# Scores of the first two batches as unsplit float32 products, two heads side by side on the array's two row halves

## The chip, the cores and the metric

One core of one Trainium2 chip runs the whole program. The metric is the device time of one execution in microseconds (us). TensorE does the matrix products (PE in the profile, and PEld for its weight loads), VectorE (DVE) and ScalarE (ACT) do everything elementwise, GpSimd (POOL) only fills a few constants, and SyncE (SP) starts the DMA transfers. The engines run at the same time and wait for each other by semaphores. TensorE's clock has two levels here, 1.2 and 2.4 GHz; the profile's PEclk column is the share of the full clock that was granted.

## The reference

Block-causal attention feeds a squared-ReLU MLP, and that feeds a soft mixture of experts. Everything is float32.

```python
# attention: 8 batches, 8 heads, 576 tokens, head size 64; blocks of 64 tokens
scores = scale * np.matmul(q, k.transpose(0, 1, 3, 2))       # scale = 1/8
scores = np.where(block_i >= block_j, scores, -1000000000.0)
scores = scores - np.max(scores, axis=-1, keepdims=True)
attn = np.exp(scores)
attn = attn / (np.sum(attn, axis=-1, keepdims=True) + 1e-09)
x = np.matmul(attn, v)            # heads side by side: 4608 tokens x 512
# MLP, 512 -> 2048 -> 512
h = np.maximum(x @ w_in, 0.0)
x = h * h @ w_out
# soft mixture of 8 experts with 4 slots each
logits = x @ phi
slot_input = softmax_over_tokens(logits).T @ x
slot_out[e] = np.maximum(slot_input[e] @ w1[e], 0.0) @ w2[e]
out = softmax_over_slots(logits) @ slot_out
```

## The kernel before

**A recorded program.** The kernel does not issue instructions as it runs. Each step is recorded by `pr.add` with the engines that may do it, a cost in ns, a due time, what it reads and writes, and the PSUM group it needs. `Program.order` then plays the program forward with these costs and fixes the order of the instructions on every engine. The order in which an engine works is thus set by this planner; how long things take is only known from the profile.

**The stages.** Tokens come in chunks of 384. A slot is one chunk by one of 16 tiles of hidden units: `slot_h` multiplies x by a tile of w_in into bank HB (PE line L898), ACT squares the ReLU, and `slot_o` multiplies by a tile of w_out into the banks O (L923, 512 columns). Later chunks use a scheme with fewer products (L1137, L1165). These products are the bulk of PE's work, and each float32 factor in them is split into a high and a low fp32r part, so that three fp32r products stand for one float32 product. The 16 weight tiles arrive as 64-bit numbers and are decoded by ACT and DVE (`w_decode`, L809 to L822, into X, WQ, W and WL).

**Attention.** Batches 2 to 7 use `job64` (L461, L516), which the change leaves as it is but for what its loads wait for. Batches 0 and 1 use `job`, once for a pair of heads (h = 0, 1; p = 0 to 3) and a list `ti` of query tiles. Tile 0 holds 64 queries, tiles 1 to 4 hold 128 each, and tile i sees the first KV[i] = 64 + 128 i keys (h = 1 has its keys in reverse order of blocks). The jobs are [0,1,2,3] of batch 0, [4] of batch 0, [0,1] of batch 1 and [2,3,4] of batch 1, four pairs each.

In a job, q and k lie with the head's 64 numbers on the 128 partitions twice, because k and q come doubled from HBM (in_qk). The split form of the scores then works like this: ACT or DVE rounds k and q/8 to fp32r (L580, L583, L584), DVE subtracts to get the rest (L587 for k on the lower 64 partitions, L590 for q), all into the lane's tile R (aR, bR), and two fp32r products of 128 rows (L621, j = 0 and 1) sum to the float32 scores of one head. The [4] jobs were `plain` already: one unsplit float32 product per head on 128 doubled rows, which the profile shows as two passes.

After the scores DVE masks a corner (L642), takes the row maximum (L644), ACT takes the exponential and its sum (L662), DVE or ACT normalises (L679, L680, L706, L707), PE transposes the probabilities (L726), ACT or DVE copies them back (L730), and PE multiplies by v (L743, L753, L761).

Two lanes hold such a job: lane a (aR, aF, PSUM banks B, four of them) and, for two pairs of batch 0 at the start, lane b (bR, bF, banks O and HB, which the MLP does not need yet). When lane b is done, `swap` gives its memory to weight tiles 4 to 15. Lane a has two sets of inputs that take turns, one in aF and one in EX:

```python
sx, rkq, V_, VD_ = L.ins[L.z]
L.z = (L.z + 1) % len(L.ins)
```

Of the kernel before, what the change touches and what calls it, by code (L numbers as in the profile page):

```python
# [7 lines left out]
F32 = mybir.dt.float32  # L8
# [39 lines left out]
class Program:  # L48
# [50 lines left out]
    def order(self, banks):  # L99
# [9 lines left out]
        modes, mode = ([], [], [], []), 0  # L109
# [158 lines left out]
def emit(tc, qk, v, vd, kq2, v2, w, phi, w1, w2, jsel, gsel, out):  # L268
# [59 lines left out]
    NF = NV + 512 + 768 + 4 * S  # L328
    late = tc.alloc_tile_pool(name="lane_b", bufs=1)
    L0, L1 = Lane(), Lane()  # L330
    for L, pl_, nm in ((L0, cp, "a"), (L1, late, "b")):
        L.name, L.w = nm, "w" if L is L0 else "w1"
        L.R = pl_.tile([128, 6 * S], F32R, name=nm + "R")
        L.F = pl_.tile([128, 9216 if L is L0 else NF], F32, name=nm + "F")
        o = NV + 512 + 768
        L.rkq = L.F[:, o:o + 4 * S].rearrange("p (h n) -> p h n", h=2)
        L.hi = [L.R[:, 2 * S * h:2 * S * h + 2 * S] for h in range(2)]
        L.ql = [L.R[:, S * (4 + h):S * (5 + h)] for h in range(2)]
# [4 lines left out]
        if L is L0:  # L343
            x = EX[:, 0:4 * S + 512 + 768]
            L.ins.append(("2", x[:, 0:4 * S].rearrange("p (h n) -> p h n", h=2),
                          x[:, 4 * S:4 * S + 512].rearrange("p (h n) -> p h n", h=2),
                          x[:, 4 * S + 512:].rearrange("p (i n) -> p i n", i=6)))
        L.nm, L.sm, L.ri = (cp.tile([128, 12], F32, name=nm + x) for x in ("nm", "sm", "ri"))

    def lane_init(L):  # L350
        for x, _, _, VD in L.ins:
            pr.add(("pool", 600, lambda VD=VD: pool.memset(VD, 0.0)), w=[(L.name, "VD" + x)], due=-1)
        pr.add(("pool", 95, lambda: pool.tensor_copy(L.R[:, 5 * S - 64:5 * S], L.VD[:, 0, 0:64])),
               r=[(L.name, "VD")], w=[(L.name, "ql", 0)], due=-1)
        pr.add(("pool", 95, lambda: pool.memset(L.sm, 1.0)), w=[(L.name, "sm", i) for i in range(12)], due=-1)
        pr.add(("pool", 95, lambda: pool.memset(L.nm, 0.0)), w=[(L.name, "nm", i) for i in range(12)], due=-1)
# [32 lines left out]
    SG = [[[[(1, 0, 0, 192, 64)], [(2, 0, 0, 320, 0)]], [[(3, 0, 0, 448, 0)]], [[(4, 0, 0, 288, 0)], [(4, 1, 288, 288, 0)]]]]  # L389
    SG.append([[[(0, 0, 0, 64, 0), (1, 0, 0, 192, 64)], [(2, 0, 0, 320, 0)]]] + SG[0][1:])  # L390

# [21 lines left out]
    def a_r():  # L413
        if not aR:
            aR.append(cp.tile([128, 6 * S], F32, name="aR2", tag="aR"))
        return aR[0]
# [8 lines left out]
    def job64(b, p, due0, due1):  # L425
# [19 lines left out]
        oldR = idle([K(nm, h) for h in range(2) for nm in ("hk", "hq", "ql")])  # L445
        oldF = idle([K("PT", x) for x in range(NPT // 64)] + [K("P", h, i, z_) for h in range(2) for i in range(5) for z_ in parts(i)])
        pr.add(("sp", 50, lambda: sp.dma_start(kq(), kq2[n2])), w=[K("kq", z)], nbytes=8 * S * 128, after=oldR)
        pr.add(("sp", 50, lambda: sp.dma_start(v_2(), v2[n2])), w=[K("v2")], nbytes=8 * S * 128, after=oldR)
# [90 lines left out]
    def job(L, b, p, ti, due0, due1, plain=False, merge=True):  # L539
# [14 lines left out]
        nq = q1 - q0  # L554
        ks = [(0, k1), (S - k1, S)]
        sc, neg = (0.0625, 2 * NEG) if plain else (1.0, 0.125 * NEG)
        pi = hd // 2
        src = qk[hd:hd + 2].rearrange("h p n -> p h n")
        whole = q0 == 0 and k1 == S
        if whole:  # L560
            pr.add(("sp", 50, lambda: sp.dma_start(rkq, src)), w=[K("rk", h) for h in range(2)] +
                   [K("rq", h) for h in range(2)], nbytes=8 * S * 128 * 2)
        else:
            for h in range(2):
                a_, e_ = ks[h]
                pr.add(("sp", 50, lambda h=h, a_=a_, e_=e_: sp.dma_start(rkq[:, h, a_:e_], src[:, h, a_:e_])),
                       w=[K("rk", h)], nbytes=4 * k1 * 128)
# [1289 lines left out]
```

## Time and profile before

| | |
|---|---|
| three runs | 1181.99, 1182.32, 1183.26 us; median 1182.32 us |
| profiled execution, its own time | 1179.87 us |
| its span in the trace | 1178.1 us |
| mean granted clock of TensorE | 0.99 |
| busy: PE, DVE, ACT | 1130.9 us (96%), 862.0 us (73%), 642.0 us (54%) |
| DMA | 265.55 MB, mean 225 GB/s |

The shares are means over stages that differ: PE is busy nearly all of the time from 140 to 1140 us, while it is the other engines that are fullest before that. So the table is to be read stage by stage, with the rows further down. The span and the execution's own time differ by 1.8 us, which lie outside the program's instructions.

### The profile page before, as it was taken

What the parts mean: (1) busy time and instruction counts of PE and PEld (TensorE: products, weight loads), DVE (VectorE), ACT (ScalarE), POOL (GpSimd) and SP (SyncE); (2) the same over time, 40 slices, a digit from 0 to 9 for tenths busy, and PEclk for the clock granted to TensorE, in tenths of its full rate; (3) what the DMA queues carried; (4) which work ended last, traced back from release to release, by engine and by line L of the source; (5) the groups of instructions that cost most, each with busy time, mean ns of one, the idle gap of its engine ahead of it and who ended that gap; (6) DMA issues with size and microseconds to landing.
All of it is one profiled execution on the core that took longest, in us unless ns stands there. A gap on an engine that the chain in (4) does not pass through costs nothing.

```text
span 1178.1 us, 28641 instructions
## 1 busy us (share of the span) xinstructions
PE 1130.9 (96%) x10918; PEld 930.9 (79%) x10918; DVE 862.0 (73%) x2464; ACT 642.0 (54%) x2047; POOL 4.1 (0%) x17
## 2 busy tenths in 40 slices
PE   5889899999999999999999999999999999999995
PEld 4677687888888888888877888888877899779843
DVE  7999988988768777887888667878888766532202
ACT  6888787666555666645554656656664000122324
POOL 1000000000000000000000000000000000000000
PEclk9899999999999999999999999999999999999998
DMA  7598637778577954665576843756653866998889
GB/s 247 177 307 254 194 118 259 236 217 255 178 221 229 315 182 134 200 196 180 175 231 216 281 150 117 223 179 202 201 184 119 293 205 196 337 391 279 292 323 322
DMA packets 145769, 265.55 MB, mean 225 GB/s; under 512 B 18784, under 2 KB 72288, under 8 KB 145632
## 3 DMA queue, kind: packets, MB, share of 16 engines
q1 hardware_dynamic: 145632, 263.73, 68.9%
q8 instruction: 86, 1.41, 0.5%
q14 instruction: 51, 0.42, 0.1%
HBM read 222.78 MB, written 40.89 MB: 224 GB/s over the span
## 4 chain that ended last, share of the span: by engine, by line
PE 79%; DVE 7%; ACT 3%; DMA 3%; issue 1%; SPq 0%; DVEq 0%; ACTq 0%
PE O L1165 17%; PE HB L898 13%; PE O L923 13%; PE HB L1137 9%; PE B L1137 6%; PE B L461 6%; PE B L516 5%; PE B L1727 1%; PE B L1333 1%; ACT aF L478 1%; PE B L1386 1%; PE O L1691 1%; PE B L726 1%; PE B L753 1%; DVE anm L644 1%
## 5 line engine op out<-in xcount | busy, mean ns | idle before, releaser
L478 ACT ACTIVATE aF<-B,aF 128x192 f32<-128x192 f32 (+8 forms) x432 | 166.1, 416 | 55.0 <-DVE aF L473 39.4
L923 PE MATMUL O<-W,MG 128*128 128x512 f32 x600 | 178.3, 399 | 0.0
L1165 PE MATMUL O<-W,MG 128*128 128x512 f32 x576 | 168.5, 398 | 0.5 <-DVE MG L1149 0.5
L898 PE MATMUL HB<-MX,W 128*128 128x384 f32 x544 | 149.5, 346 | 4.3 <-ACT R L904 3.8
L471 DVE TENSOR_REDUCE aF<-B 128x1 f32<-128x192 f32 (+8 forms) x432 | 109.9, 315 | 39.2 <-PE B L461 37.9
L923 PEld LDWEIGHTS O<-W,MG 128*128 128x128 f32 x600 | 110.3, 188 | 19.7 <-issue 2.3
L1165 PEld LDWEIGHTS O<-W,MG 128*128 128x128 f32 x576 | 106.0, 188 | 22.8 <-issue 2.5
L898 PEld LDWEIGHTS HB<-MX,W 128*128 128x128 f32 x544 | 98.3, 189 | 13.1 <-ACT R L904 5.5
L508 DVE STREAM_TRANSPOSE aF<-aF 128x448 f32<-128x448 f32 (+8 forms) x216 | 98.4, 488 | 0.0
L478 ACT ACTIVATION_READ_ACCUMULATOR aF<-B,aF 128x1 f32 x432 | 98.2, 228 | 0.0
L904 ACT ACTIVATE R<-HB 128x384 f32<-128x384 f32 x96 | 47.6, 496 | 83.7 <-PE HB L898 80.9
L1165 PE MATMUL O<-WL,MG 128*128 128x512 f32 x288 | 89.3, 397 | 0.0
L923 PE MATMUL O<-WL,MG 128*128 128x512 f32 x264 | 77.7, 396 | 0.0
L461 PE MATMUL B<-aR 64*32 64x192 f32 (+8 forms) x3456 | 77.5, 302 | 0.0
L898 PE MATMUL HB<-MX,WL 128*128 128x384 f32 x224 | 76.9, 343 | 0.5 <-DVE WL L822 0.4
L461 PEld LDWEIGHTS B<-aR 64*32 64x32 f32 x3456 | 53.7, 105 | 27.2 <-issue 8.7
L898 PE MATMUL HB<-MXe,W 128*128 128x384 f32 x256 | 72.5, 343 | 0.6 <-ACT R L904 0.5
L907 DVE CAST MG<-R 128x384 fp32r<-128x384 f32 x73 | 26.0, 356 | 62.6 <-ACT R L905 61.8
L504 ACT ACTIVATE aF<-aF 128x256 f32<-128x256 f32 (+8 forms) x162 | 58.7, 432 | 19.3 <-DVE aF L498 19.3
L516 PEld LDWEIGHTS B<-aF,aR 64*64 64x64 f32 x1728 | 52.8, 133 | 17.3 <-issue 4.7
L516 PE MATMUL B<-aF,aR 64*64 64x192 f32 (+8 forms) x1728 | 65.3, 301 | 0.0
L1165 PEld LDWEIGHTS O<-WL,MG 128*128 128x128 f32 x288 | 53.9, 188 | 13.6 <-issue 1.9
(361 smaller groups left out, 2184.6 us busy)
## 6 DMA issues: line engine op xcount, KB each, us to landing
W<-ws_d SPq DMA_DIRECT2D x200, 256.0 KB, 3.3
WL<-wlo_d SPq DMA_DIRECT2D x83, 512.0 KB, 4.2
WL<-wlo_d SPq DMA_DIRECT2D x96, 256.0 KB, 3.0
aR<-in_kq SPq DMA_DIRECT2D x24, 576.0 KB, 4.6
aR<-in_v SPq DMA_DIRECT2D x24, 576.0 KB, 3.9
ws_d<-EX SPq DMA_DIRECT2D x16, 512.0 KB, 5.8
Wr<-in_w SPq DMA_DIRECT2D x16, 512.0 KB, 5.1
xt_d<-aF SPq DMA_DIRECT2D x8, 768.0 KB, 5.0
```

The source lines that it names most:

```text
L461: pe.matmul(bank(gs[h])[32 * g:32 * g + 32, c:c + 32 * i + 32].rearrange("p (b n) -> p b n", n=32), x[:, S + 64 * i + 32 * q_:S + 64 * i + ...
L471: pr.add(("dve", c_tt(n), lambda g=gs[h], n=n, c=c, x=x: dve.reduce_max(St[:, 0, x:x + 1], bank(g)[:, c:c + n], axis=AX.X, negate=True)), ...
L478: pr.add(("act", c_act(n, ext=2), lambda g=gs[h], n=n, c=c, x=x, i=i, h=h: act.activation(P_(i)[:, h], bank(g)[:, c:c + n], AF.Exp, bias=S ...
L504: act.activation(P_(i)[:, h], P_(i)[:, h], AF.Copy, scale=fct[:, x + h:x + h + 1])
L508: pr.add(("dve", c_tr(2 * n), lambda i=i: dve.transpose(P_(i), P_(i))), w=[K("P2", i, h) for h in range(2)])
L516: pe.matmul(bank(gs[q_])[64 * h:64 * h + 64, 32 * k:288].rearrange("p (i n) -> p i n", n=32), v_2()[sl, h, 64 * k:64 * k + 64], L0.F[sl, o ...
L898: pr.add(("pe", c_mm(CH), lambda a=a, b_=b_, sl=sl, n=n, k=k: pe.matmul(HB[:, 0:CH], (wl() if a == "l" else W[ft])[:, sl], b_(c, k), start ...
L904: pr.add(("act", c_act(CH), lambda: act.activation(r_, HB[:, 0:CH], AF.Relu)), w=["HB", ("r", j)], due=-1)
L907: pr.add([("dve", c_cp(CH), lambda: dve.tensor_copy(gh, r_)), ("act", c_act(CH, True), lambda: act.copy(gh, r_))], r=[("r", j)], w=[("gh", ...
L923: pr.add(("pe", c_mm(512), lambda a=a, b_=b_, sl=sl, t=t, p_=p_: pe.matmul(OB[t], a[:, sl], (wl() if b_ == "l" else W[ft])[:, 512:1024], s ...
L1137: pr.add(("pe", c_mm(CH), lambda a=a, b_=b_, k=k, fst=fst, lst=m == 5: pe.matmul((bank(g) if g else HB)[:, 0:CH], W[r][:, a + 128 * k:a + ...
L1165: pr.add(("pe", c_mm(512), lambda a=a, lo_=lo_, sl=sl, t=t, p_=p_: pe.matmul(OB[t], a[:, sl], wo(n) if lo_ else W[ft][:, 512:1024], start= ...
```

## The change

The split form is gone. For batches 0 and 1 the two heads of a pair now lie one above the other, head 0 on partitions 0 to 63 and head 1 on 64 to 127 (in_qk is no longer doubled), and each score tile is one float32 product per head with 64 rows, the two heads right after each other into two PSUM banks. Tile 0 uses 64 rows by 64 columns of the array, tiles 1 to 4 use 64 rows by 128 columns; `mode` 3 and 4 tell the planner of these. The scale of 1/8 moves into the exponential, so every group of maxima gets a small multiplication by 0.125, and tile 0 has its maximum and its exponential taken for each head apart, on 64 rows. The tiles aR and bR are gone; aR is now only `job64`'s input tile and exists from the start, so that the first loads of `job64` (in_kq, in_v) wait for nothing. Lane a gets a third set of inputs. The [4] jobs of batch 0 and the [0,1] jobs of batch 1 are recorded in turns (one pair of each), where all four [4] came first. A [4] job takes all four banks of its pool in one step, the other groups of tiles take two.

```diff
-        modes, mode = ([], [], [], []), 0
+        modes, mode = ([], [], [], [], []), 0
...
+def c_mm64(n):
+
+    return max(115.0, n / 0.6 + 5)
...
-        L.R = pl_.tile([128, 6 * S], F32R, name=nm + "R")
-        L.rkq = L.F[:, o:o + 4 * S].rearrange("p (h n) -> p h n", h=2)
+        L.rkq = L.F[:, o:o + 2 * S]
...
+            L.ins.append(("3", EX[:, 4 * S + 128:6 * S + 128], L.F[:, 8384:8896].rearrange("p (h n) -> p h n", h=2),
+                          L.F[:, 7616:8384].rearrange("p (i n) -> p i n", i=6)))
...
-        pr.add(("sp", 50, lambda: sp.dma_start(kq(), kq2[n2])), w=[K("kq", z)], nbytes=8 * S * 128, after=oldR)
-        pr.add(("sp", 50, lambda: sp.dma_start(v_2(), v2[n2])), w=[K("v2")], nbytes=8 * S * 128, after=oldR)
+        pr.add(("sp", 50, lambda: sp.dma_start(kq(), kq2[n2])), w=[K("kq", z)], nbytes=8 * S * 128, after=())
+        pr.add(("sp", 50, lambda: sp.dma_start(v_2(), v2[n2])), w=[K("v2")], nbytes=8 * S * 128, after=())
...
-        for h in () if plain else range(2):
-            raw, hi = rkq[:, h], L.hi[h]
-            a_, e_ = ks[h]
-            pr.add(cpy(hi[:, a_:e_], raw[:, a_:e_], k1), r=[K("rk", h)], w=[K("hk", h)], cls="hi")
-            pr.add(cpy_s(hi[:, S + q0:S + q1], raw[:, S + q0:S + q1], nq), r=[K("rq", h)], w=[K("hq", h)], cls="hi")
-            pr.add(sub(hi[64:128, a_:e_], raw[64:128, a_:e_], f(hi[64:128, a_:e_]), k1),
-                   r=[K("rk", h)], w=[K("hk", h)], cls="kl")
-            pr.add(sub_s(L.ql[h][:, q0:q1], raw[:, S + q0:S + q1], f(hi[:, S + q0:S + q1]), nq),
-                   r=[K("rq", h), K("hq", h)], w=[K("ql", h)], cls="ql")
...
+        def scores(gs, pieces):
+            def mm(ps):
+                for g, (i, c0, n, bc) in ps:
+                    for h in range(2):
+                        x, k0 = rkq[64 * h:64 * h + 64], (S - KV[i]) * h + c0
+                        rows = slice(0, 128) if i else slice(64 * h, 64 * h + 64)
+                        pe.matmul(bank(g[h])[rows, bc:bc + n], x[:, S + Q0[i]:S + Q0[i] + QW[i]], x[:, k0:k0 + n],
+                                  start=True, stop=True)
...
+        for ph_ in ([0, 1], [2], [3], [4]):
...
+            if tiles == [4]:
+                gs = [[Group(L.w) for _ in range(2)] for _ in range(2)]
+                scores(gs, [(4, 0, 288, 0), (4, 288, 288, 0)])
...
+            else:
+                gs = [Group(L.w) for _ in range(2)]
+                scores([gs] * len(tiles), [(i, 0, KV[i], 64 if i == 1 else 0) for i in tiles])
...
     for p in range(4):
         d = t_at(0) + 5 * p - 10
-        job(L0, 0, p, [4], d, d + 8.0, 1)
-    for p in range(4):
-        d = t_at(0) + 5 + 3 * p
-        job(L0, 1, p, [0, 1], d, d + 8.0, 0)
+        job(L0, 0, p, [4], d, d + 8.0)
+        job(L0, 1, p, [0, 1], d + 3, d + 11.0)
```

The planner makes a new order of everything from this. Three places show it. The first is the start of TensorE's program. Before, lanes a and b (aR, bR) take turns with split products: each line stands for a product with the high or the low part of q.

```order
L621 MATMUL B_69<-aR 128x192
L621 MATMUL B_70<-aR 128x320
L621 MATMUL B_71<-aR 128x64
L621 MATMUL B_69<-aR 128x192
L621 MATMUL B_70<-aR 128x320
L621 MATMUL B_71<-aR 128x64
L621 MATMUL O_65<-bR 128x192
```

After, the products read the loaded inputs themselves (aF, bF), head 0 and head 1 of a tile in successive lines and in different banks.

```order
L574 MATMUL B_69<-aF 64x64
L574 MATMUL B_70<-aF 64x64
L574 MATMUL B_69<-aF 128x192
L574 MATMUL B_70<-aF 128x192
L574 MATMUL O_65<-bF 64x64
L574 MATMUL O_66<-bF 64x64
L574 MATMUL O_65<-bF 128x192
L574 MATMUL O_66<-bF 128x192
L574 MATMUL B_71<-aF 128x320
L574 MATMUL B_72<-aF 128x320
```

Nothing stands ahead of the first score now but the loads, and tile 0 has moved to the front.

The second place is VectorE's program behind the last row maxima of the first two pairs (TENSOR_REDUCE) and ahead of the last normalisation of their probabilities (TENSOR_SCALAR on aF, 448 wide). Before, the split of the second two pairs (EX for lane a, bF for lane b) stands there:

```order
L644 TENSOR_REDUCE bnm<-O_66 128x1
L580 CAST aR<-EX 128x448
L580 CAST bR<-bF 128x448
L584 TENSOR_SCALAR aR<-EX 128x448
L587 TENSOR_TENSOR aR<-EX,aR 64x448
L668 TENSOR_SCALAR ari<-asm 128x1
L587 TENSOR_TENSOR bR<-bF,bR 64x448
L668 TENSOR_SCALAR bri<-bsm 128x1
L674 RECIPROCAL ari<-ari 128x1
L590 SCALAR_TENSOR_TENSOR aR<-EX,aR 128x448
```

After, the decoding of the first weight tile (X) stands in their place:

```order
L654 TENSOR_SCALAR bnm<-bnm 128x2
L769 TENSOR_SCALAR X_0_93<-X_0_93 128x512
L769 TENSOR_SCALAR X_1_94<-X_1_94 128x512
L614 TENSOR_SCALAR ari<-asm 128x2
L770 TENSOR_SCALAR X_0_93<-X_0_93 128x512
L616 RECIPROCAL ari<-ari 128x2
L770 TENSOR_SCALAR X_1_94<-X_1_94 128x512
L621 TENSOR_SCALAR aF<-aF,ari 128x448
```

So the splits have left the queue and the weights have moved up in it.

The third place is SyncE's queue of loads, from the first weight tile on (YA, call). Before:

```order
L790 DMA YA<-in_w 128x1024
L790 DMA call<-in_w 128x1024
L566 DMA aF<-in_qk 128x576 x2
L568 DMA aF<-in_qk 128x2x128
L1514 DMA J<-in_jsel 96x64
L576 DMA EX<-in_vd 64x3x64
L566 DMA EX<-in_qk 128x576 x2
L568 DMA EX<-in_qk 128x2x128
L790 DMA YA<-in_w 128x1024
```

After, further down in the same stretch, the first three loads of `job64` (aR) stand ahead of the second weight tile:

```order
L554 DMA aF<-in_qk 64x192 x2
L550 DMA bF<-in_qk 128x576
L556 DMA bF<-in_qk 128x448
L556 DMA aF<-in_qk 128x192
L444 DMA aR<-in_kq 128x1152
L445 DMA aR<-in_v 128x1152
L444 DMA aR<-in_kq 128x1152
L563 DMA aF<-in_vd 64x64
L1468 DMA J<-in_jsel 96x64
L746 DMA YA<-in_w 128x1024
```

The loads of q and k are halved in size, and `job64`'s have moved to the start of the program.

## Rows read from the trace of the kernel before

**Rows 1.** Windows: stretch, its us, busy us (instructions) by engine, PEclk, DMA share, GB/s.

```profile
0.00:20.00 20.00, 9.37 (x48) 8.54 (x49) 13.64 (x55) 13.28 (x37) 4.08 (x17) 1.00 0.92 297
20.00:60.00 40.00, 32.63 (x227) 24.47 (x226) 39.30 (x114) 34.26 (x92) 0.00 (x0) 0.87 0.56 173
60.00:140.00 80.00, 70.66 (x442) 56.99 (x442) 75.63 (x217) 65.71 (x174) 0.00 (x0) 0.98 0.81 262
140.00:240.00 100.00, 98.19 (x796) 81.22 (x802) 88.10 (x232) 78.02 (x204) 0.00 (x0) 1.00 0.59 195
240.00:1000.00 760.00, 757.18 (x8203) 636.56 (x8184) 594.09 (x1726) 400.79 (x1431) 0.00 (x0) 1.00 0.65 203
```

**Rows 2.** What PE waited for, 0 to 140 us: total, times, longest.

```profile
PE B L621 <- ACT aR L583: 8.8, 2, 8.5
PE B L621 <- ACT aF L662: 2.9, 6, 1.3
PE B L726 <- ACT aF L662: 2.8, 1, 2.8
PE B L726 <- DVE aF L679: 2.1, 1, 2.1
```

**Rows 3.** Windows of tile aR alone; PE, PEld, DVE, ACT, POOL.

```profile
20.00:60.00 40.00, 4.41 (x16) 2.81 (x16) 4.01 (x8) 0.00 (x0) 0.00 (x0) 0.87 0.56 173
60.00:140.00 80.00, 9.47 (x51) 7.23 (x51) 11.46 (x26) 8.84 (x22) 0.00 (x0) 0.98 0.81 262
```

**Rows 4.** The same for tile bR.

```profile
20.00:60.00 40.00, 4.32 (x16) 2.81 (x16) 3.25 (x6) 0.00 (x0) 0.00 (x0) 0.87 0.56 173
```

**Rows 5.** Timeline of the start: start us, us, instruction, idle before and releaser.

```profile
5.68 0.56 ACT L580 CAST aR<-aF 128x448 fp32r<-128x448 f32 x1 [1.23 <-DMA aF<-in_qk]
...
7.82 1.04 ACT L583 ACTIVATE aR<-aF 128x448 fp32r<-128x448 f32 x2 [1.01 <-DMA aF<-in_qk]
...
8.45 1.68 PE L621 MATMUL B<-aR 128*128 128x192 f32 x6 [8.45 <-ACT aR L583]
...
10.87 0.35 DVE L644 TENSOR_REDUCE anm<-B 128x1 f32<-128x192 f32 x1
```

**Rows 6.** Small DVE instructions, 0 to 240 us: busy us, mean ns, idle before.

```profile
L655 DVE TENSOR_SCALAR anm<-anm 128x1 f32<-128x1 f32 x16 | 3.3, 207 | 0.1
```

**Rows 7.** Timeline of PE: split and unsplit score products in a row.

```profile
33.42 0.27 PE L621 MATMUL B<-aR 128*128 128x192 f32 x1
33.53 0.27 PE L621 MATMUL HB<-bR 128*128 128x192 f32 x1
...
33.95 0.31 PE L621 MATMUL B<-aR 128*128 128x320 f32 x1
34.10 0.31 PE L621 MATMUL O<-bR 128*128 128x320 f32 x1
...
35.06 0.36 PE L621 MATMUL B<-aR 128*128 128x448 f32 x1
35.26 0.36 PE L621 MATMUL O<-bR 128*128 128x448 f32 x1
...
83.21 2.10 PE L621 MATMUL B<-EX 128*128 128x288 f32 x8
```

**Rows 8.** The chain that ended last: `job64`'s product with v, 64x64 tiles.

```profile
296.73 2.64 PE B L516 x72
```

**Rows 9.** Timeline of PE around a change of the array's tile size.

```profile
75.17 0.33 PE L898 MATMUL HB<-MX,WL 128*128 128x384 f32 x1
75.34 0.34 PE L898 MATMUL HB<-MX,W 128*128 128x384 f32 x1
75.61 1.09 PE L753 MATMUL B<-aF,EX 128*64 128x128 f32 x16
76.63 0.49 PE L761 MATMUL B<-aF,EX 128*128 128x128 f32 x2
```

**Rows 10.** DMA rate, 0 to 45 us in 40 slices of 1.125 us.

```profile
GB/s 0 68 341 209 341 338 361 336 290 307 363 340 334 183 347 405 404 400 358 72 70 193 15 0 51 313 22 29 197 348 247 181 185 262 38 76 186 68 288 23
```

More of the change, by code (lines that the diff above doesn't have):

```diff
@@ L352, in lane_init @@
             pr.add(("pool", 600, lambda VD=VD: pool.memset(VD, 0.0)), w=[(L.name, "VD" + x)], due=-1)
[L353 to L356, printed above, removed]
+        pr.add(("pool", 95, lambda: pool.memset(L.sm, 1.0)), w=[(L.name, "sm", i, h) for i in range(12) for h in range(2)], due=-1)
+        pr.add(("pool", 95, lambda: pool.memset(L.nm, 0.0)), w=[(L.name, "nm", i, h) for i in range(12) for h in range(2)], due=-1)
     def p_col(h, i):
@@ L414, in a_r @@
         if not aR:
-            aR.append(cp.tile([128, 6 * S], F32, name="aR2", tag="aR"))
+            aR.append(cp.tile([128, 6 * S], F32, name="aR"))
         return aR[0]
@@ new lines, in job @@
+        rd = [K("rk", 0), K("rk", 1), K("rq")]
+        nm2_, sm2_, ri2_ = (x.rearrange("p (h i) -> p h i", h=2) for x in (L.nm, L.sm, L.ri))
+        def scores(gs, pieces):
[6 more added lines that the diff above has]
+                                  start=True, stop=True)
+            ps = list(zip(gs, pieces))
+            on = [x for x in ps if x[1][0] == 0], [x for x in ps if x[1][0]]
+            fst = True
+            for md, y in zip((3, 4), on):
+                if y:
+                    pr.add(("pe", sum(c_mm64(x[1][2]) for x in y), lambda y=y: mm(y)), r=rd, grp=[x for g in gs for x in g] if gs[0] is not gs[-1] else gs[0],
+                           take=fst, mode=md,
+                           after=idle([K("P", h, i, z) for h in range(2) for i, _, _, _ in pieces for z in parts(i)]) if fst else ())
+                    fst = False
@@ L689, in job, with nmk, smk, invert @@
+        def nmk(tiles):
+            return [K("nm", 6 * (h if i else 1) + i + z, 0 if i else h) for i in tiles for h in range(2) for z in parts(i)]
+        def smk(tiles):
+            return [K("sm", 6 * (h if i else 1) + i + z, 0 if i else h) for i in tiles for h in range(2) for z in parts(i)]
+        def invert(tiles):
             lo, hi_ = tiles[0], tiles[-1] + 1
-            hs = [(h, i, z) for h in range(2) for i in tiles for z in parts(i)]
-            sm2_, ri2_ = (x.rearrange("p (h i) -> p h i", h=2) for x in (L.sm, L.ri))
@@ L699, in job @@
-            pr.add(("dve", 80, lambda lo=lo, hi_=hi_: dve.reciprocal(ri2_[:, :, lo:hi_], ri2_[:, :, lo:hi_])), w=[K("ri", ph_)])
-            for h in range(2):
-                for i in tiles:
-                    if i == 0 and h == 0:
-                        continue
+                                                                    ALU.add, ALU.add)), r=smk(tiles), w=[K("ri", lo)])
+            else:
+                pr.add(("dve", 75, lambda: dve.tensor_scalar_add(ri2_[:, :, lo:hi_], sm2_[:, :, lo:hi_], 1e-9)), r=smk(tiles),
+                       w=[K("ri", lo)])
@@ L704, in job @@
+            pr.add(("dve", 80, lambda: dve.reciprocal(ri2_[:, :, lo:hi_], ri2_[:, :, lo:hi_])), w=[K("ri", lo)])
+            for i in tiles:
+                for h in range(2) if i else (1,):
                     P_ = L.F[:, p_col(h, i):p_col(h, i) + KV[i]]
@@ L710, in pk @@
         def pk(h, i):
[L711 to L712 removed]
+            return [K("P", x, i, z) for x in range(2) if i == 0 or h in (x, 2) for z in parts(i)] + ([K("P", 0, 1, 0)] if i == 0 else [])
         for gi, g, bats, at in plan(ti):
+            at = {x: o + (1152 if ti == [0, 1] else 0) for x, o in at.items()}
             for bt in bats:
@@ L1006, in prep @@
                    r=[("W", ft, 0), lk + (0,)], w=[("st", nm)], due=due,
-                   after=idle([("a", n_, h) for n_ in ("rk2", "rq2") for h in range(2)] + [("a", "V2"), ("a", "VD2")]))
+                   after=idle([("a", "rk" + x, h) for x in "23" for h in range(2)] + [("a", "rq2"), ("a", "rq3"), ("a", "V2"), ("a", "VD2")]))
         s1, s2, s3, s4 = (S_[:, 256 * j:256 * j + 256] for j in range(4))
```

208 lines of the change are left out of this document (70 added, 138 removed).

## Prediction

> **What bounds the kernel now.** I read the windows first, to see which engine is full in which stage [rows 1]. From 240 to 1000 us PE is busy 757.2 of 760 us, so what is gained or lost earlier simply shifts that stage. What can change lies in the first 240 us, where PE idles 29.1 us: 10.6 in the first 20, 7.4 from 20 to 60, 9.3 from 60 to 140 and 1.8 from 140 to 240. In those stages VectorE is busy 98.3% (39.30 of 40 us), 94.5% (75.63 of 80) and 88.1% (88.10 of 100) from 20 us on. PE's idle share goes with it: 18.4%, 11.7%, 1.8%. So until 140 us VectorE sets the pace, and PE fills what it is let. The waits of PE say the same [rows 2]: the first score waits 8.5 us for the rounding of its inputs on ACT (L583), and later waits name exponentials (L662) and normalisations (L679), which stand behind VectorE's queue.
>
> What fills VectorE is partly the splitting of q and k: on the lanes' tiles aR and bR it works 4.01 + 3.25 us from 20 to 60 us and 11.46 us from 60 to 140 [rows 3, 4].
>
> **The start.** The first score waits for three loads one after the other and their rounding: a third load of 224 KB (128 x 448 floats) is there at 5.7 us, with 672 KB asked for so far, the 448 KB of q at 7.8 us with 1344 KB asked for, and PE starts at 8.45; VectorE, which still splits, takes the first maximum at 10.87 [rows 5]. After the change the queue begins with k of lane a and of lane b (288 KB each) and q of lane a (224 KB): 800 KB. Between the two landings that is 5.7 + 2.1 x 128/672 = 6.1 us, and no rounding follows, so PE starts at about 6.2. Tiles 0 and 1 come first: 0.43 us at the pace worked out below, but products take about twice as long there now (six split ones in 1.68 us [rows 5], where the pace gives 0.74 and a tail of 0.2), so some 1.3 us with a tail, and the first maximum lies at 7.5: **3.3 us earlier**. I take VectorE's date, since its queue of maxima paces what comes next. PE's start alone would give 2.2, which is the lower bound.
>
> **VectorE.** The splits go: 7.26 us from 20 to 60, 11.46 from 60 to 140, and 5.2 later by the same view. New are 24 small multiplications and minima of the maxima and 8 more row maxima, counted in the new order. They cost what the present small ones do, 207 ns each [rows 6], 6.6 us in all; I put 1.9, 3.3 and 1.4 us into the three stages. VectorE's work becomes 39.30 - 7.26 + 1.9 = 33.9 us in what is now 20 to 60, and 75.63 - 11.46 + 3.3 = 67.5 us in what is now 60 to 140. ACT loses 8.84 us of rounding from 60 to 140 [rows 3] and was not full there (65.71 of 80 us, [rows 1]).
>
> **TensorE's work.** Split products of 192, 320 and 448 columns follow each other in 0.11, 0.15 and 0.20 us, and a head needs two. Unsplit, eight passes of 288 columns take 2.10 us with a tail of 0.17 (a product of 448 columns lasts 0.36 and the next begins after 0.20), so 0.24 a pass, or 0.84 ns a column; a head needs two passes [rows 7]. If the two heads run at the same time on their halves of the array, a pair costs: [0,1,2,3] 1.72 us instead of 2.19, [4] 0.97 instead of 1.93 (it was unsplit already, head after head), [0,1] 0.43 instead of 0.77, [2,3,4] 2.26 instead of 2.47. Four pairs of each: 21.5 us instead of 29.4.
>
> Do the halves run at the same time? No score product of before shows it, but `job64`'s product with v does, with four tiles of 64 rows and 64 columns: 1440 columns each, two passes, would take 4 x 1440 x 2 x 0.84 ns = 9.7 us one after the other, and the row says 2.64 [rows 8]. I take full overlap, the bound from the other side is none. The Trainium skill (TensorE: Matmul & The Clock Gate, section "Measured speedup vs the span model") gives 3.07 for four row tiles, 77% of the ideal; at that share two tiles would give about 1.53, by estimate 28 us for these scores, and the total would come out some 5 us later. The row gives 9.7/2.64 = 3.7 of 4, so the trace doesn't bear this out for 64-row tiles.
>
> Against this stand changes of the array's tile size. An MLP product that follows another begins 0.17 us after it, the first product on half the columns 0.27 us after it; the way back costs about as much (16 of them from 75.61 in 1.09 us, then 76.63) [rows 9]. So 0.095 each. Counted over PE's order up to the last of these scores there are 49 such changes before and 89 after, 29 of the new ones behind the first MLP product: 1.0 us before it, 2.8 after it, at no cost where PE waits anyway.
>
> By stage, with the jobs where the trace has them: PE's work becomes 32.63 - 2.8 + 1.0 = 30.8 us for 20 to 60, 70.66 - 3.7 + 1.8 = 68.7 for 60 to 140, and 98.19 - 0.4 + 0.9 = 98.7 for 140 to 240.
>
> **Loads.** q and k are halved, 1.5 instead of 3.0 MB for four jobs of a pair, and three loads of `job64`, 576 KB each, move up ahead of the second weight tile. They take 5 us at 340 GB/s; the rate lies under 80 GB/s in seven of the nine slices from 21 to 32 us [rows 10], so they are hidden there, and the second weight tile waits for the decoding of the first in any case. If that cover were gone, 5 us of delay of one weight tile would be the price. The third input set lets the next pair load earlier; I give it nothing.
>
> **The sum.** What PE's idle share will be I read from a line through two stages of before: 1.8% where VectorE is busy 88.1%, 11.7% where it is busy 94.5%. (At 98.3% the line gives 17.6%, and the first stage had 18.4%.) A stage then lasts as long as its PE work and its share of idle time make it. For 20 to 60: at 35.5 us VectorE is busy 95.5%, the line says 13.2%, and 30.8/0.868 is 35.5: **4.5 us less**. For 60 to 140: at 73.8 us VectorE is busy 91.5%, the line says 7.0%, and 68.7/0.93 is 73.9: **6.2 less**. For 140 to 240: 98.7/0.982 = 100.5: **0.5 more**. Together 3.3 + 4.5 + 6.2 - 0.5 = 13.5 us. The profiled execution took 1179.9 us, 2.4 less than the median of the three runs; the forecast is 1166.4 against the one and **1169 us** against the other.
>
> What I leave out: the clock is granted at 0.87 from 20 to 60 and 0.98 from 60 to 140 [rows 1], which with the two levels of 1.2 and 2.4 GHz is about 10 and 3 us at the lower one, each time after PE stood still. With fewer stops some of it may go; at most about 5 us of PE time comes back.
>
> **Rivals.**
> *Everything goes to PE.* PE idles 1.8% from 60 us on and the low-clock stretches vanish: another 4 + 5 us, 1160 us. For it: the stage after 140 us does run so. Against it: VectorE is still over 90% busy.
>
> *Banks.* A [4] job now takes all four banks of lane a at once, and nothing else of lane a (transposes, products with v) gets one until its exponentials end. The longest wait of a score on an exponential now is 1.3 us [rows 2]; eight [4] tiles at 1.3 us are 10 us, and with the 13.5 that leaves 1179 us. For it: the row with 2.8 us, where transposes wait for exponentials. Against it: the MLP's products have banks of their own and fill such gaps after the first 60 us. The Trainium skill (TensorEngine Tiling (Array Packing), "Gotcha 1: PSUM Pressure") says that row tiles must write to different banks and so raise the need for them; no run here shows yet what that costs.
>
> *The halves take turns.* If the two heads run one after the other, the scores cost 43 us instead of 21.5. PE would then have about 4 us more in 20 to 60, 10 in 60 to 140 and 5 in 140 to 240; VectorE would be no limit, 78.7/0.982 = 80 us for the second of these, and the start's gain would go in the slower scores: 0 + 1 + 0 - 5, about 4 us slower, 1186 us. It decides once more than two thirds of the overlap is missing. The 2.64 us speak against it.
>
> *It does nothing.* Weight tiles, not scores, might be what VectorE and the loads are late with: the gain of the start is then given back in waits for weights, 1181 us. Against it: decoding uses the same full VectorE.
>
> **Chances.** The forecast (1163 to 1174) 0.6; everything to PE 0.15; banks 0.13; halves in turn 0.06; nothing 0.06. Two runs of this kernel differ by up to 0.1%, and 0.2% (2.4 us) is about what can be told from no change. Faster by more: 0.6 + 0.15 + 0.11 = 0.86; within it 0.06; slower 0.08. The range reaches from the first rival to the second: 1160 to 1178.
>
> **What would show it.** The first score at 6.2 us and the first maximum at 7.5. Score products of the two heads starting within 0.02 us of each other, a pair of 448 columns done in 0.75 us. VectorE at 90 to 95% until about 127 us with PE idle 7 to 13%. The first MLP product some 7 to 8 us earlier than now. The stage from 240 us on unchanged in length. I am wrong if score pairs take twice that, if PE waits over 1 us for banks at each [4], or if ACT stands waiting for a weight tile among the first exponentials, where the new order puts it.

## The result: 9.5 us faster, with the working of the forecast only half right

The changed kernel takes 1172.62 us (median of four, 1171.15 to 1174.47), the kernel before 1182.15 us beside it (four, 1181.82 to 1183.26): a ratio of 0.9919, 95% interval 0.9901 to 0.9936, or 9.5 us (0.8%) less. The forecast was 1169 us, range 1160 to 1178. The profiled execution took 1172.62 us with a span of 1170.8, against 1179.87 and 1178.1, so the two traces hold 7.3 of the 9.5 us.

The windows after, in the same columns as [rows 1]:

```profile
0.00:20.00 20.00, 10.96 (x40) 6.05 (x41) 11.82 (x54) 10.38 (x34) 3.94 (x16) 0.80 0.84 249
20.00:60.00 40.00, 33.64 (x236) 23.84 (x235) 34.75 (x114) 31.86 (x95) 0.00 (x0) 0.80 0.60 187
60.00:140.00 80.00, 74.58 (x477) 56.75 (x475) 69.65 (x206) 61.68 (x164) 0.00 (x0) 0.98 0.69 229
140.00:240.00 100.00, 99.49 (x824) 81.46 (x825) 89.35 (x242) 72.71 (x193) 0.00 (x0) 1.00 0.59 191
240.00:1000.00 760.00, 756.95 (x8149) 634.61 (x8148) 592.15 (x1714) 399.32 (x1428) 0.00 (x0) 1.00 0.65 203
```

VectorE fell as wanted, from 39.30 to 34.75 us between 20 and 60 and from 75.63 to 69.65 between 60 and 140. PE's idle time fell too, but in 20 to 60 only from 7.4 to 6.4 us. The clock is new: 0.80 in the first two rows, where 1.00 and 0.87 were recorded (the 1.00 is too high, as e7 shows below).

The waits of PE up to 140 us, beside [rows 2]:

```profile
PE B L574 <- ACT aF L597: 5.4, 5, 1.4
PE B L574 <- DMA aF<-in_qk: 5.1, 1, 5.1
PE HB L854 <- ACT R L860: 1.8, 3, 0.7
PE B L682 <- DVE aF L621: 1.7, 1, 1.7
```

The 8.5 us for the rounding have become 5.1 us for the load alone. Scores (L574) that wait for exponentials (L597), because those still hold the banks, are up from 2.9 to 5.4 us.

The start, beside [rows 5], from the timelines of PE, VectorE and ACT:

```profile
5.14 1.42 PE L574 MATMUL B<-aF 64*64 64x64 f32 x8 [5.14 <-DMA aF<-in_qk]
...
6.67 0.22 DVE L588 TENSOR_REDUCE anm<-B 64x1 f32<-64x64 f32 x1 [6.67 <-PE B L574]
...
8.59 1.28 ACT L597 ACT_TABLE_LOAD   x1 [8.59 <-DVE anm L654]
9.89 0.31 ACT L597 ACTIVATE aF<-B,anm 64x64 f32<-64x64 f32 x1
...
14.22 0.66 ACT L765 ACTIVATE X<-YA 128x512 f32<-128x512 f32 x1 [0.94 <-DMA YA<-in_w]
```

The first score stands at 5.14 us, the first maximum at 6.67, both sooner than forecast. What nobody had priced is the third row. Before, ACT's first instruction was a rounding, and its table load lay at 0.73 us under the first loads; now the first instruction of ACT is an exponential, and the load of 1.28 us stands in its queue, in front of it and behind its wait for VectorE.

A pair of heads by itself, two places of PE's timeline at the full clock:

```profile
79.19 1.24 PE L574 MATMUL B<-aF 64*128 64x288 f32 x8
80.36 0.44 PE L854 MATMUL HB<-MX,W 128*128 128x384 f32 x1
...
114.21 1.02 PE L574 MATMUL B<-EX 64*128 64x448 f32 x4
115.16 1.19 PE L879 MATMUL O<-W,MG 128*128 128x512 f32 x4
```

A whole [4] takes 1.17 us to the next product, 448 columns take 0.95, each with a change of tile size in and out. The forecast was 0.97 and 0.75 plus 0.19. The halves do work at the same time.

**Where the 8 us are.** The first product of MLP slot 30 starts at 277.4 us before and 269.1 after; the rest of the program is as long as it was (900.7 and 901.7 us). I split the time up to there, with windows of 1 us, into PE's idle time, what the low clock adds (busy time x (1 - granted clock)) and the rest, called work here. The granted clock as the profile records it leaves out the low clock at the very start (shown at e7 below), so a part of the work column is low clock too:

| up to slot 30, us | idle | low clock | work | sum |
|---|---|---|---|---|
| before | 29.1 | 6.5 | 241.7 | 277.4 |
| after | 21.3 | 10.4 | 237.3 | 269.1 |

The work fell by 4.4 us. The forecast has 29.4 - 21.5 us of scores less 3.8 us of new tile-size changes, 4.1. That the two lie so close is partly luck, since the work column holds the low clock of the start. Idle time fell by 7.8. The low clock took 3.9 back. By date the gain does not lie where the forecast put it: the first MLP product starts at 59.9 us instead of 60.2, slot 10 at 140.7 instead of 146.9, slot 30 at 8.3 us less. By stage that is 0.3 us gained where the sum had 7.8, then 5.9 for 6.2, then 2.1 where the sum had 0.5 lost.

### The profile page after: what moved, and what is told of

Read it like the earlier page. It is cut to its first block, busy times and chain, and to the rows that moved or that the text cites. A ratio compares the mean times of both kernels' runs of the same rounds, so it can differ in the third digit from the quotient of the medians.

```text
span 1170.8 us, 28546 instructions
## 1 busy us (share of the span) xinstructions
PE 1132.3 (97%) x10918; PEld 921.0 (79%) x10918; DVE 845.1 (72%) x2443; ACT 623.6 (53%) x2015; POOL 3.9 (0%) x16
## 4 chain that ended last, share of the span: by engine, by line
PE 82%; DVE 8%; ACT 4%; DMA 3%; issue 1%; SPq 0%; ACTq 0%; DVEq 0%
PE O L1121 18%; PE HB L854 15%; PE O L879 14%; PE HB L1093 9%; PE B L1093 7%; PE B L458 6%; PE B L513 5%; DVE anm L588 1%; PE B L1681 1%; DMA XR<-in_w 1%; PE B L1289 1%; PE B L1342 1%; ACT aF L597 1%; PE O L1645 1%; PE B L682 1%
## 5 line engine op out<-in xcount | busy, mean ns | idle before, releaser
L505 DVE STREAM_TRANSPOSE aF<-aF 128x64 f32<-128x64 f32 (+8 forms) x216 | 98.0, 487 | 0.0
L458 PEld LDWEIGHTS B<-aR 64*32 64x32 f32 x3456 | 53.8, 106 | 27.4 <-issue 9.9
```

The source lines that it names most:

```text
L458: pe.matmul(bank(gs[h])[32 * g:32 * g + 32, c:c + 32 * i + 32].rearrange("p (b n) -> p b n", n=32), x[:, S + 64 * i + 32 * q_:S + 64 * i + ...
L505: pr.add(("dve", c_tr(2 * n), lambda i=i: dve.transpose(P_(i), P_(i))), w=[K("P2", i, h) for h in range(2)])
```

## Experiments

Each was timed beside the kernel before on its own chip. "Lost" is the difference of its ratio to 0.9919, times 1181.5 us. Single executions of one kernel differ by up to 0.7% (the kernel before: 1178.0 to 1186.7 us in 74; the 0.1% of the prediction came from three), so a difference under 3 us between two of these kernels is not certain. Dates, waits and splits come from the one profiled execution of each kernel, and these spread too: those of e2 and e6 are the slowest of their kernels (1181.98 and 1187.50 us), those of e12 and e13 are among the fastest (1172.11 and 1171.71). The planner makes a new order for every edit; only e3, e8 and e12 keep the changed kernel's order row by row.

| kernel | median us | ratio, 95% interval | lost, us | idle / low clock / work up to slot 30 |
|---|---|---|---|---|
| changed kernel | 1172.62 | 0.9919 (0.9901, 0.9936) | 0 | 21.3 / 10.4 / 237.3 |
| e1 no turns | 1176.92 | 0.9959 (0.9943, 0.9976) | 4.7 | 21.5 / 9.8 / 241.1 |
| e2 two sets | 1177.95 | 0.9970 (0.9958, 0.9982) | 6.0 | 28.1 / 12.7 / 237.0 |
| e6 neither | 1183.07 | 1.0011 (0.9998, 1.0024) | 10.9 | 27.4 / 18.7 / 237.1 |
| e7 VectorE's splits back | 1181.59 | 0.9997 (0.9987, 1.0006) | 9.2 | 24.0 / 9.5 / 243.2 |
| e11 ACT's rounding back | 1176.82 | 0.9957 (0.9944, 0.9971) | 4.5 | 20.3 / 10.9 / 239.6 |
| e8 scores twice | 1183.63 | 1.0010 (0.9999, 1.0021) | 10.8 | 15.6 / 5.5 / 257.8 |
| e3 table load early | 1172.13 | 0.9918 (0.9898, 0.9939) | -0.1 | 20.8 / 6.5 / 238.2 |
| e12 products in the gaps | 1175.30 | 0.9940 (0.9922, 0.9958) | 2.5 | 17.6 / 5.4 / 244.6 |
| e5 more such products | 1178.76 | 0.9974 (0.9960, 0.9988) | 6.5 | 17.4 / 9.4 / 246.5 |
| e9 lane b first | 1173.99 | 0.9930 (0.9915, 0.9946) | 1.3 | 21.1 / 11.4 / 236.7 |
| e10 better start | 1177.05 | 0.9954 (0.9937, 0.9970) | 4.1 | 19.2 / 13.6 / 240.7 |
| e13 raw tile elsewhere | 1176.01 | 0.9954 (0.9941, 0.9968) | 4.1 | 19.1 / 8.6 / 239.2 |

### Turns and the third input set

```diff
# e1
-        job(L0, 1, p, [0, 1], d + 3, d + 11.0)
+    for p in range(4):
+        d = t_at(0) + 5 + 3 * p
+        job(L0, 1, p, [0, 1], d, d + 8.0)
# e2: the line L.ins.append(("3", ...)) goes; e6: both edits
```

> The changed kernel with the two kinds of jobs one after the other again (the four [4] jobs, then the four [0,1] jobs with their old due times). In the changed kernel the first MLP product stands at 59.9 us, no earlier than before, and it waits for lane b's last job, whose last products lie at 58.9. Theory A (turns put [0,1] work of lane a ahead of lane b's end): the first MLP product comes 2 to 4 us earlier, at 56 to 58, and the total is 1170 to 1173 us. Theory B (the low clock decides, 27 us of it in the first 125 us against 14 before): it moves only if the low stretches shorten by over 5 us. Theory C (turns are a good part of the gain, because a [4] job alone holds all four banks of lane a): 1176 to 1180 us, with PE waiting 1.3 us at each of the [4] jobs.

> The changed kernel with two input sets for lane a instead of three. The prediction gave the third set nothing: then 1171.5 to 1174 us. If the earlier loads of the third set are part of the 9.5 us gained, some 1 to 3 us are lost, 1174 to 1176 us, and a score of a [4] or [0,1] job waits for its load.

> The changed kernel without turns and without the third input set, so that of the change the float32 products side by side are left. The prediction's sum of 13.5 us counted only these. Theory V (the freed VectorE and PE carry the gain, turns and third set only matter together with what else they move): 1173 to 1177 us. Theory W (the stage from 60 us hangs on weight tile 3, whose load waits for lane b's end, and on loads; the cheaper scores alone are lost in that wait, and turns with 4.3 us and the third set with 5.3 us are nearly the whole gain, adding up): 1179 to 1183 us, and a wait of ACT for XR of over 3 us between 60 and 80.

e1: the first MLP product did come sooner, at 58.4 us, 1.5 us for the 2 to 4 of theory A, but the total is the one of theory C. The waits that theory C named did not come with it: scores wait for exponentials four times and 3.7 us in all, less than in the changed kernel. e2: the price I had put at nothing is 6.0 us. e6: with the float32 products, and what else of the change stays in it (`job64`'s early loads, four banks at once for a [4]), the gain is gone (1.0011), though VectorE and PE have been relieved in full. Two windows of e6, PE's waits in e6 up to 240 us, and PE's waits in e2 up to 140:

```profile
60.00:140.00 80.00, 71.02 (x433) 55.43 (x431) 65.84 (x195) 55.56 (x150) 0.00 (x0) 0.89 0.67 214
120.00:134.50 14.50, 11.68 (x45) 8.25 (x47) 11.43 (x42) 7.78 (x25) 0.00 (x0) 0.53 0.70 237
```

```profile
PE B L572 <- DMA aF<-in_qk: 7.4, 2, 5.6
PE B L572 <- ACT aF L595: 4.4, 2, 3.7
...
PE B L572 <- DMA EX<-in_qk: 1.9, 1, 1.9
```

```profile
PE HB L852 <- ACT R L858: 5.8, 1, 5.8
...
PE B L715 <- DMA aF<-in_vd: 3.1, 1, 3.1
```

VectorE is at 82% in e6 (65.84 of 80), and PE still idles 9 us, as it did before the change with VectorE at 94.5%. Two waits are for inputs of lane a that come late (1.9 us of EX, 1.8 of the 7.4 for aF), and the scores wait 3.7 us for exponentials at one place. In e2 it is a product with v that waits 3.1 us for its input; of the scores only the very first waits for a load there. The 5.8 us are another matter: ACT's squared ReLU (L858) stood in the queue behind a decoding step that waited for weight tile 3,

```profile
69.72 0.66 ACT L763 ACTIVATE X<-XR 128x512 f32<-128x512 f32 x1 [7.41 <-DMA XR<-in_w]
70.28 0.47 ACT L858 ACTIVATE R<-HB 128x384 f32<-128x384 f32 x1
```

from ACT's timeline of e2. In the changed kernel the wait for weight tile 3 is 1.5 us long, and in e6 it is 2.2, so the mark that theory W set for e6 (over 3 us) did not come, only its total.

Idle time is not all that e6 has more of. Up to slot 30 it idles 6.1 us more than the changed kernel, and 8.3 us more are put down to the low clock. A good part of those lies from 120.0 to 134.5 us, where the granted clock is 0.53 and neither VectorE (11.43 of 14.50) nor ACT (7.78) is full. Whether the low clock cost time there no run shows.

### The relief of VectorE, of ACT and of PE, each taken back

```diff
# e7 (e11: act.copy instead of dve.tensor_sub)
+ for y, n in ((a_, min(k1, 512)), (S + q0, q1 - q0)):
+     pr.add(("dve", c_tt(n), lambda ...: dve.tensor_sub(accs[sl, 0:n], rkq[sl, y:y + n], rkq[sl, y:y + n])), r=rd, w=["scr"])
# e8
-                    for h in range(2):
+                    for h in (0, 1, 0, 1):
```

> The changed kernel with VectorE's share of the splitting put back as bare work: per head of a job other than [4] one subtraction over k's columns (cut at 512) and one over q's, whose results nobody reads. About 6.5 us of VectorE per stage before 60 us and 11 us from 60 to 140, nothing added on PE or ACT and no wait for it except by the reloads of the inputs. Theory V (VectorE's queue paced 20 to 140 us): 5 to 10 us slower than the changed kernel, 1178 to 1182 us, VectorE over 93% from 20 to 140. Theory W (weights and loads pace): 1173 to 1176 us.

> The changed kernel with ACT's share of the rounding put back as bare copies of k's and q's columns, which nobody reads, for all jobs but [4]: about 8 us more work on ACT before 60 us and 6 to 140. The sum priced this relief at nothing. If VectorE alone mattered: 1173 to 1175 us. If any engine's relief counts, since lane b's and lane a's steps pass through both in turn: 1178 to 1182 us, with ACT over 85% busy from 20 to 60.

> The changed kernel with every pair of score products issued twice (same inputs, same place, so the second writes what the first wrote): what it would cost if the halves of the array took turns. That is about 21 us more PE work at the high clock, 4 in the first 20 us, 4 to 60, 8 to 140 and 5 behind. The prediction's rival gave 1186 us. Theory V: the part behind 60 us counts in full, 13 us, and the part before mostly hides in waits for exponentials: 1184 to 1190 us. If PE has room until 125 us (theory W): 1178 to 1182 us. The low clock of 12 to 22 and 39 to 53 us should shrink, since PE stands still less.

e7 loses 9.2 us: theory V, though in an order that is new from the start on (the first exponential at 14.15 us for 9.89, lane a's scores of tile 3 from 15.28 for 10.74). Two windows of e7:

```profile
20.00:60.00 40.00, 35.35 (x235) 25.09 (x235) 37.25 (x131) 33.22 (x92) 0.00 (x0) 0.83 0.46 142
60.00:140.00 80.00, 71.52 (x441) 53.93 (x440) 78.22 (x225) 64.01 (x171) 0.00 (x0) 0.94 0.76 243
```

From 60 to 140 us VectorE is at 98% (78.22 of 80), and PE idles 8.5 us instead of 5.4. Before 60 us nothing was lost: the first MLP product is at 58.7 us, although the new order let ACT wait for its first weight tile until 13.6 us. The loss came between slots 2 (3.4 us ahead of the changed kernel) and 8 (7.5 behind). From 60 to 140 us the granted clock is 0.94, where it was 0.98, so a part of what VectorE's added work cost may have come by way of the clock.

The split puts most of e7's loss under work (243.2 for 237.3), though no product was added. That is low clock at the start, which the recorded clock does not show. Three transposes in a row, in the changed kernel where it grants 0.50, and in e7 where it grants 1.00, early and later:

```profile
20.02 0.85 PE L682 MATMUL B<-ident,aF 128*128 128x128 f32 x3
```

```profile
22.21 0.85 PE L687 MATMUL B<-ident,aF 128*128 128x128 f32 x3
...
30.62 0.51 PE L687 MATMUL B<-ident,aF 128*128 128x128 f32 x3
```

At 22.21 us e7 takes as long as the changed kernel does at the lower level. By the pace of its products PE runs at the lower level from its first product up to about 24 us in e7, up to about 14 us in the kernel before (a split product of 192 columns is followed by the next after 0.21 us at 12.28, and after 0.11 at 33.42 [rows 7]) and up to about 8.7 us in the changed kernel. As an estimate (half of PE's busy time up to there) that is 2.7 us of low clock before and 1.8 after which stand under work; with them the work fell by 3.5 us and the low clock took 3.0.

e11 loses 4.5, between its two cases; ACT was 90% busy from 20 to 60 (36.09 of 40). The sum had priced ACT's relief at nothing. e8 says what the overlap is worth: 10.8 us, between what theories W and V had given. It adds 20.5 us of work and gets 5.7 back in idle time and 4.9 in clock: PE fills its own gaps, and in this run, where PE stands still less, its clock is low for less time.

### The clock, the start and the way to lane b's end

```diff
# e3
+    pr.add(("act", 1300, lambda: act.activation(L0.ri[:, 5:6], L0.sm[:, 5:6], AF.Exp)), r=[("a", "sm", 5, 0)], due=-1)
# e12, behind the scores of the last tile 3 and the two halves of the first [4]
+                    for _ in range((12 if i == 3 else 10) if pads else 0):
+                        pe.matmul(bank(g[1])[:, 448:512], ident, ident[:, 0:64], start=True, stop=True)
# e9
-        lane_b += job(L1, 0, 2 * n + 1, [0, 1, 2, 3], 15.0 * n, 15.0 * n + 15, n > 0)
+        lane_b += job(L1, 0, 2 * n + 1, [0, 1, 2, 3], 9.0 * n, 9.0 * n + 15, n > 0)
# e13 (with e3), in raws()
+        if ft == 2 and j == 0:
+            return (lambda: u(EX[:, 3584:4608])), [("part", 0), ("part", 1)]
```

> The changed kernel with one exponential of a single column at the very start, so that ACT's table load (1.28 us at 8.6 us, ahead of the first real exponential at 9.9) lies under the first loads again. PE's order stays what it is. If ACT's queue at the start sets what follows (theory D): first exponential at 8.6 us, the first transposes 1 us earlier, the first MLP product 0.8 to 1.3 us earlier, total 1171.3 to 1172 us. If lane b's end or the clock decides (theories A, B): the exponential is earlier and the first MLP product moves by less than 0.4 us, total within 0.5 us of the changed kernel.

> The changed kernel with 32 products of 64 columns that nobody reads, on PE at three places between 35 and 42 us where it waits for banks or normalisations (12 behind the last score of tile 3, 10 and 10 behind the two halves of the first [4] job); everything else in the same order. Accounting up to the first product of MLP slot 30: idle 21.3, loss by the low clock 10.4, work at the high clock 237.3 us. If standing still there is what drops the clock for 39 to 53 us, and the low clock is part of the shortfall: the low stretch shrinks by over 6 us, loss by the clock 2 to 4 us less, total 1169 to 1171.5 us. If the low clock only fills time in which PE would wait anyway: loss smaller, idle larger by as much, total 1172 to 1174 us.

e3: the first exponential is at 8.80 us instead of 9.89, but ACT then waits 1.62 us instead of 0.94 for the weight tile that it decodes between the exponentials, and the first exponential of tile 2 is at 15.03 instead of 15.35. In the profiled execution the first MLP product is 1.4 us sooner; the total does not show it.

e12 tests the clock in the same order. Stretches of the changed kernel and of e12:

```profile
12.00:22.00 10.00, 7.39 (x24) 4.64 (x22) 9.91 (x45) 9.03 (x29) 0.00 (x0) 0.51 0.93 281
22.00:40.00 18.00, 14.58 (x113) 8.79 (x111) 15.70 (x51) 12.19 (x42) 0.00 (x0) 0.97 0.54 169
40.00:53.00 13.00, 10.16 (x43) 7.44 (x43) 12.29 (x39) 11.41 (x30) 0.00 (x0) 0.50 0.52 149
53.00:60.00 7.00, 6.90 (x72) 5.64 (x72) 4.76 (x16) 6.26 (x19) 0.00 (x0) 0.99 0.77 257
```

```profile
40.00:53.00 13.00, 9.66 (x86) 8.09 (x86) 12.87 (x42) 12.04 (x33) 0.00 (x0) 1.00 0.50 142
```

The clock from 40 to 53 us goes from 0.50 to 1.00, the clock's part of the split from 10.4 to 5.4 us, and the first MLP product moves by 0.3 us (59.55 for 59.88). Slot 30 is 1.5 us sooner in the profiled execution, but the timed ones gain nothing (lost 2.5, with overlapping intervals). VectorE is 99% busy there (12.87 of 13), and was 94.5% before the added products. But the added products also put other work off. From the chain of e12:

```profile
35.96 2.84 PE HB L578 x24
...
42.87 3.91 DMA YA<-in_w
...
46.80 0.67 ACT X L768
```

The load of YA goes out at 42.87 us where it was 41.92, and the decoding behind it (ACT X) is at 46.80 where it was 45.96 (the chain of the changed kernel is shown further down). From there to the first MLP product it is 12.75 us in e12 and 13.92 in the changed kernel. So, as an estimate from these rows, the full clock gave back about 1.2 us, of the 5.0 that the split puts down to the clock; the rest went into PE's waits for VectorE and ACT, which are nearly full there. The total, 1175.30, lies above both cases that were set for it. The low clock from 40 to 53 us is thus not the cause of the 7.5 us that are missing by the first MLP product; what the one from 12 to 22 us costs, no run shows by itself.

> The changed kernel with products that nobody reads on PE: 20 transposes of the identity before the first score, 12 after the first jobs' last scores, 12 ahead of the first [4] job's scores and 28 in two later places of the same stage, put where PE waits. Theory B (low clock ate the missing 4 us): the low stretches of 12 to 22 and 39 to 53 us shrink from 24 to under 12 us, the first MLP product comes 2 to 4 us earlier, total 1168 to 1171 us. Theory A: PE is faster there but waits for ACT and VectorE all the same; first MLP product within 1 us of 59.9 and the total 1172 to 1175 us, since the added products cost up to 0.2 us per four.

> The changed kernel with lane b's second job due 6 us sooner (9 instead of 15), so that its last transposes and products stand ahead of lane a's. Theory W: lane b ends at 54 to 56 us instead of 58.9, the load of weight tile 3 (XR, issued at 59.9 before) goes out 3 to 5 us sooner, the first MLP product follows, and the total is 1168 to 1171 us. Theory V: the end comes sooner but lane a's work is only put off; total 1172 to 1174 us.

> The changed kernel with a better start, three things together: ACT's table load under the first loads, the decoding of weight tile 0 held back behind the exponentials of tile 2 (in the changed kernel ACT waits 0.94 us for that weight tile between exponentials, and 1.62 where the table load is early), and 14 transposes of the identity on PE ahead of the first score so that its clock is high by then. If the start paces lane b's end: exponentials of tile 2 end 2 to 3 us sooner (at about 14.5 instead of 17.4), first MLP product 1 to 2 us sooner, clock loss up to slot 30 no larger, 1169 to 1171.5 us. If a gain of 1 or 2 us at the start is absorbed before 60 us, as for the table load alone: 1171.5 to 1174 us.

e5 lost 6.5 us: its products at the start made the planner put lane b's scores first, and the first exponential came at 11.71 us, so it tells little. e9 brought lane b's last products forward and the first MLP product stayed: lost 1.3, theory V. From PE's timeline in the changed kernel, then in e9:

```profile
58.75 0.39 PE L717 MATMUL O<-bF 128*128 128x128 f32 x2
...
59.88 0.42 PE L854 MATMUL HB<-MX,W 128*128 128x384 f32 x1
```

```profile
56.50 0.49 PE L717 MATMUL O<-bF 128*128 128x128 f32 x2
...
59.67 0.42 PE L854 MATMUL HB<-MX,W 128*128 128x384 f32 x1
```

e10 lost 4.1. Its exponentials of tile 2 ended at 16.35 us instead of 17.41, 1.1 us sooner and not the 2 to 3 that were meant, its clock loss was larger (13.6), and its first MLP product came at 61.9 us; what the start gained was gone before 60 us, in an order that is new as well.

> The changed kernel with the early table load and with one half of the raw weight tile 2 loaded into columns 3584 to 4608 of EX, which are free until 130 us, instead of YA. In the changed kernel the chain of work runs at 42 to 47 us over the load of YA (4.0 us, issued at 41.92 once VectorE has used up what it held) to the decoding step on ACT (L765 at 45.96) and the copies of lane b that stand behind it in ACT's queue, and from there to lane b's end at 58.9 and the load of weight tile 3 at 59.9. If that link sets lane b's end: the step stands at 43 us or before, the first MLP product 1.5 to 4 us sooner, total 1168 to 1171 us. If lane b's and lane a's own steps through ACT, VectorE and PE take as long without it: first MLP product within 1 us of the 58.5 of the kernel with the early table load, and 1171.5 to 1173.5 us.

The chain of work of the changed kernel from 38 us on, and that of e13 (start us, us, what):

```profile
39.12 0.59 DVE WL L778
39.79 0.66 DVE X L769 x2
41.30 0.57 DVE X L772
41.92 4.01 DMA YA<-in_w
45.96 0.67 ACT X L765
46.63 0.48 ACT bF L686
...
59.91 5.66 DMA XR<-in_w
```

```profile
39.04 1.34 ACT aF L597 x4
40.38 0.86 ACT bF L597 x3
41.40 0.21 ACT bF L597
41.61 1.11 ACT aF L622 x2
42.72 1.56 ACT bF L622 x3
44.29 0.56 ACT X L767
44.85 1.04 ACT bF L686 x2
...
58.35 5.00 DMA XR<-in_w
```

The load of YA is gone from the chain, and ACT's exponentials, normalisations and copies of both lanes stand in its place, almost as long: lane b's copy is 1.8 us sooner, the first MLP product at 58.1 against 58.5 with the early table load alone. That is the second case. The profiled execution (1171.71) is the fastest of five up to 1177.10, and the median is 4 us worse than e3's, which this doesn't explain.

None of these is a version that is certainly better than the changed kernel; e3 is as good.

## Why the prediction was right and where not

**Right.** The overlap of the halves and the price of tile-size changes: 1.17 and 0.95 us for 1.16 and 0.94 worked out, 4.4 us less PE work for 4.1 (3.5 with the low clock of the start taken out, by the estimate above). The start: 4.2 us by the first maximum for 3.3. VectorE's queue is a limit, as far as e7 with its new order shows. The stage behind 240 us is unchanged. "Halves take turns" has the price it was given in kind: e8 ends level with the kernel before, where the rival had 4 us more. "Banks" has a price, but not the 10 us that it was given: scores wait 5.4 us for exponentials where it was 2.9, and over 1 us at two of the eight jobs with a tile 4 (ahead of 36.82 and 39.93, and ahead of 118.61), not at each.

**The step that failed** is "What PE's idle share will be I read from a line through two stages of before". From 20 to 60 us VectorE is busy 86.9%, below both points of the line, and PE idles 15.9%. From 60 to 140 us VectorE is busy 87.1% (69.65 of 80), where the line gives 0.3%, and PE idles 6.8%. The mean over the first of these stages hid what it is made of: VectorE is 99% busy from 12 to 22 us and 94.5% from 40 to 53, with ACT at 90% and 88%, and has room in between and after (15.70 of 18 and 4.76 of 7). The work that left VectorE left it mostly where it was not the last to finish. So of 3.3 + 4.5 us up to the first MLP product 0.3 arrived. That product stands in PE's order behind lane b's last products at 58.75, which have passed through VectorE, ACT and PE many times. No single one of these holds it: in e9 lane b's last products come 2.2 us sooner and it stays at 59.7, and in e13 a link of the chain that is cut (4.0 us of load) is replaced by the next.

**The second** is "The third input set lets the next pair load earlier; I give it nothing"; the turns were not priced either. Both together are the whole gain, 10.9 us (e6; 4.7 and 6.0 one by one), and so are VectorE's relief (9.2, e7) and the overlap (10.8, e8). These three do not add up: taken back one at a time, the parts lose 9.2 + 10.8 + 6.0 + 4.7 + 4.5 = 35 us of a gain of 9.5. My reading is that each takes away a limit behind which the others stand: with cheap scores but two sets, lane a's next inputs are late and PE idles; with three sets and the old load on VectorE the inputs wait in line. The rival "It does nothing" is, in its total, what the priced part of the change does alone; not by its reason, since ACT's waits for weight tiles in XR are 2.7 us in e6 and 3.4 in the changed kernel.

So the total came out near the forecast by luck: the sum was 4 us too high, what it counted gives nothing alone, and two parts that it had left out made up for that. Luck are also the 5.9 us for 6.2 from the first MLP product to slot 10: e6 has what the sum counted and gains nothing between these two dates (92.3 us for 86.7 before). The sentence on ACT waiting for a weight tile among the first exponentials came true (0.94 us), and e3 and e10 say that it was not what decided.

**Open.** How the pieces of the chain up to 58.9 us would have to be shortened together for the first MLP product to come sooner; and why e10 and e13, which did what they were meant to do locally or in part, are 4 us slower. New orders of the planner may differ by that much by themselves, so e1, e2 and e11 with 4.5 to 6 us are less certain than e6, e7 and e8. That inputs arriving late are what the third set mends is read from the waits of e2 and e6, not from an experiment on loads alone. The low clock of e6 from 120.0 to 134.5 us is a rival to it. And no run takes back `job64`'s early loads or the four banks at once, which stay in e6.

## What to carry to other kernels

When several engines are nearly full, a part taken off one of them is worth what the next limit leaves, so price a change by asking what is late next in each short stretch, and not by a line through means of long stages. Buffers that let the next job begin sooner are a part of such a change and need a price of their own: here the cheaper scores were worth nothing without them. And a split of time into idle, low clock and work is a way to find a question, not an answer: where another engine was full, taking the low clock away gave back about 1 us of the 5 that the split had put down to it.

## What was unexpected of the hardware

The place of ACT's table load (1.28 us each time): at 0.73 us before, and in e3, e7, e10 and e11, although the first real instruction behind it waits, in e7 until 13.58 us for a transfer; but at 8.59 us in the changed kernel and 10.42 in e5, where the first instruction is an exponential that waits for VectorE. Why the load waits along in the one case and not in the other the runs don't show; one dummy exponential ahead of it is enough to move it.

In the changed kernel TensorE's clock fell after PE had stood still: it was at 0.51 from 12 to 22 us, after a wait of 1.30 us ahead of 10.74, and at 0.50 from 40 to 53 us after waits of 1.38 and 1.34 us ahead of 36.82 and 39.93; 32 products of 64 columns put into these last gaps held it at 1.00. At the start of the program the recorded clock is not to be trusted: it is 1.00 up to the first fall that is recorded, while transposes in e7 take as long as at 0.50 (0.85 us for three, at 22.21 us).
